# Where ScalarE and VectorE read the keys of two urgent searches in an attention and mixture-of-experts kernel

## The chip, the cores and the metric

The kernel runs on one core of one Trainium2 chip. The metric is the device time of one execution in microseconds (us). A core has engines that each work off their own instructions in order and wait for one another through semaphores: TensorE (PE; its weight loads are PEld), VectorE (DVE), ScalarE (ACT), GpSimd (POOL) and SyncE (SP), which issues transfers. SBUF is the large memory on the core, PSUM the small one into which TensorE writes its sums.

## The reference

Three layers follow one another:

```python
a = softmax(causal(q @ k.T / 8)); local = a @ v            # 4 batches, 8 heads, 576 rows, 64 columns
mem_out = (phi(q) @ M_prev) / (phi(q) @ z_prev + 1e-6)     # phi(x) = elu(x) + 1
x = g * mem_out + (1 - g) * local                          # 2304 tokens of 512

logits = x @ w_gate                                        # 8 experts
for idx in argsort(-logits.flatten()):                     # greedy, best pair of token and expert first
    tok, e = idx // 8, idx % 8
    if assigned[tok] >= 0 or counts[e] >= 288: continue    # each expert takes 2304 / 8 tokens
    assigned[tok] = e; counts[e] += 1
out[assigned == e] = relu(x[mask] @ w1[e]) @ w2[e]         # per expert, 512 -> 1024 -> 512

out = (silu(x @ w_gate2) * (x @ w_val)) @ w_out            # 512 -> 1536 -> 512
```

The greedy assignment is what the change is about: which expert fills up first, and with which 288 tokens, has to be known before that expert's products can start.

## The kernel before, in words

**The attention** fills the first 250 us. Then come eight routings, one for each expert in the order in which the experts fill up; each is followed by the expert's products, and after every 512 tokens the last layer runs for that group of tokens (four groups of 512 and one of 256).

**A routing** (`route`, from L990) takes each token's wish (its best open expert), turns the 18 x 8 values so that 8 rows per expert hold 160 keys each (`vb`, `kx`, L1009 to L1022), and searches the 288th largest key of each expert. The search goes by digits of base 4, 16 rounds, eight on the upper 16 bits of the key (`t.h[1]`, L1035) and eight on the lower ones; between the halves (L1094) the lower bits (`t.h[0]`, L1039) are added to what is left of the upper ones. In a round three thresholds are tried: ScalarE counts for the first with a Sign (L1050, L1052; result in `sg`), VectorE for the other two (L1060, L1063; result in `cn`); TensorE adds up the counts over the rows of an expert (L1076, L1077, with `grp` and `ngrp`); VectorE compares with 288 and adds the digit (L1081) to what was found. After 16 rounds the key is turned on TensorE (L1110), the expert that is full first is chosen, the ranks of its tokens are found (L1139 to L1207), and TensorE makes the list of token numbers (L1217), with which GpSimd gathers the tokens (`xg`, L1273) and the weights (`r`).

**The urgent searches** are those of routings 0 and 1 (`near`, which `HARDS = 2` sets). They have their own form. The keys lie in PSUM, in the tile `rp` (`t.pk`, 512 columns of 4 bytes, which is one bank): the keys in columns 0 to 159, what is left of them in the second half in 256 to 415, TensorE's sums from column 480. VectorE counts from there with the digits found so far as an operand (L1060), so that no threshold has to be made first. ScalarE cannot take thresholds in that way; so in each round but the last of a half it copies the keys with the sign turned and the next threshold added (L1071) from `rp` to one of the two SBUF tiles that the keys would otherwise take, and its next Sign (L1050) reads that copy. Rounds 0 and 8 have no found digits: VectorE (L1063) and ScalarE's Sign (L1052) both read `rp`.

**What sets the order.** A planner (`schedule`) takes operations with estimated durations and dependencies and works out one order for each engine, before anything runs. The operations of the urgent searches are marked as hard: others may be put ahead of them on an engine only if they end in time by the estimates. Between them the planner puts other work. In the first search there are only conversions of the last layer's weights from 64-bit floats (`from64`): ScalarE makes two parts (L434, L440), VectorE shifts one (L442) and puts the sign to it in two halves (L445), GpSimd adds (L448). 34 of these remain after the attention. In the second search there are also the products of expert 0 (L1255): the turning of its tokens (L1486, L1489, L1491), the splitting of weights into a high and a low part (`ws`: ScalarE L1284, then VectorE or GpSimd L1288), and `hd` (L1517, L1519). Ahead of expert 0 stand four groups of products that only keep TensorE busy (L1300).

[...]

Of the kernel before, what the change touches and what calls it, by code (L numbers as in the profile page):

```python
# [74 lines left out]
def kernel(ctx: ExitStack, tc: tile.TileContext, qt_, kt_, v, M_prev, z_prev, beta,  # L75
# [910 lines left out]
    def route(ph, prev):  # L986
# [6 lines left out]
        def step(eng, dur, fn, deps=(), **kw):  # L993
            last[0] = Op(None, {eng: dur}, fn, deps=[last[0]] + list(deps), hard=ph < HARDS, **kw)
            return last[0]
# [29 lines left out]
        def f(e):  # L1025
            t.h = [rt.tile([128, 160], F32, name=f"h{x}") for x in range(3)]
            t.kd = rt.tile([128, 2], F32, name="kd")
            t.junk = rt.tile([128, 160], BF, name="junk")
            t.jk2 = rt.tile([128, 160], BF, name="jk2")
            t.kj = rt.tile([128, 16], F32, name="kj")  # L1030
            if near:

                ptile()
                t.pk, t.hs, t.h[1] = t.p, list(t.h), t.p[:, 0:160]
            A.activation(t.h[1], t.kx.bitcast(U16).rearrange("p (c b) -> p b c", b=2)[:, 1], AF.Copy)  # L1035
            t.R = t.h[1]
        near, sk, base = ph < HARDS, rp(), None
# [5 lines left out]
        for rd in range(16):  # L1043
            sp_ = sk if near else rp()
            past = near and rd % 8 > 0

            def f(e, rd=rd, past=past):
                with nc.allow_low_precision(reason="whole numbers up to 160"):
                    if past:
                        A.activation(t.jk2, t.xs, AF.Sign, bias=gain[:, rd, 3:4], accum_out=sgns[rd % 2])  # L1050
                    else:
                        A.activation(t.jk2, t.R, AF.Sign, scale=-1.0, bias=t.th[:, 0:1] if rd % 8 else steps[:, rd, 0:1],  # L1052
                                     accum_out=sgns[rd % 2])
            sgn = Op(None, {"A": 0.49}, f, deps=[last[0], base], hard=near, lat=SAFE if ph else 0.0, slack=RND if ph else 0.0,
                     use=[sk] if near and not past else [])

            def f(e, rd=rd, past=past):
                for j in (1, 2):
                    if past:
                        V.scalar_tensor_tensor(t.junk, t.R, gain[:, rd, 3:4], steps[:, rd, j:j + 1].to_broadcast([128, 160]),  # L1060
                                               op0=OP.subtract, op1=OP.is_ge, accum_out=cnts[rd % 2][:, j:j + 1])
                    else:
                        V.tensor_scalar(t.junk, t.R, t.th[:, j:j + 1] if rd % 8 else (j + 1) * 4.0 ** (7 - rd), None,  # L1063
                                        op0=OP.is_ge, op1=OP.add, accum_out=cnts[rd % 2][:, j:j + 1])
            cnt = step("V", 0.8 if past else 0.74 if rd % 8 else 0.6, f, lat=SAFE if ph else 0.0, slack=RND if ph else 0.0,
                       use=[sk] if near else [])
            if near and (rd + 1) % 8:

                def f(e, rd=rd):
                    t.xs = t.hs[1 + rd % 2]  # L1070
                    A.activation(t.xs, t.R, AF.Copy, scale=-1.0, bias=4.0 ** (6 - rd) - (0.5 if rd < 8 else 2.0 ** -17))  # L1071
                base = Op(None, {"A": 0.24}, f, deps=[sgn], hard=True, use=[sk])

            def f(e, rd=rd):
                t.p = t.pk[:, 480 + 16 * (rd % 2):] if near else ptile()
                PE.matmul(t.p[:, 0:4], grp, cnts[rd % 2], start=True, stop=False)  # L1076
                PE.matmul(t.p[:, 0:1], ngrp, sgns[rd % 2], start=False, stop=True)  # L1077
            step("PE", 0.08, f, deps=[sgn], take=[] if near else [sp_], use=[sk] if near else [])

            def f(e, rd=rd):  # L1080
                V.scalar_tensor_tensor(t.kj[:, 0:4], t.p[:, 0:4], float(CAP), gain[:, rd], op0=OP.is_ge, op1=OP.mult,  # L1081
                                       accum_out=gain[:, rd + 1, 3:4] if (rd + 1) % 8 else t.kd[:, 1 - rd // 8:2 - rd // 8])
            step("V", 0.17, f, use=[sp_])
            if (rd + 1) % 8 and not near:
                def f(e, rd=rd):
                    t.th = rt.tile([128, 4], F32, name="th", bufs=2)
                    V.tensor_scalar(t.th[:, 0:3], steps[:, rd + 1], gain[:, rd + 1, 3:4], None, op0=OP.add, op1=OP.add,
                                    accum_out=t.th[:, 3:4])
                step("V", 0.22, f)
            elif rd == 7:  # L1090
                def f(e):
                    if near:
                        t.h[2] = t.pk[:, 256:416]
                    V.scalar_tensor_tensor(t.h[2], t.h[1], t.kd[:, 1:2], t.h[0], op0=OP.subtract, op1=OP.add)  # L1094
                    t.R = t.h[2]
                step("V", 0.35 if near else 0.25, f, deps=[low_], port="" if near else "V", use=[sk] if near else [])

        def f(e):
            t.key = rt.tile([128, 2], U16, name="key")
# [550 lines left out]
```

## Time and profile before

| what | value |
|---|---|
| three runs | 1043.67, 1036.31, 1039.59 us, median 1039.59 |
| the profiled execution | 1039.32 us |
| its span, first to last instruction | 1037.6 us |
| TensorE, matmuls | busy 923.2 us, 89% of the span |
| VectorE | busy 783.5 us, 76% |
| ScalarE | busy 598.6 us, 58% |
| GpSimd | busy 312.2 us, 30% |
| granted TensorE clock, mean | 0.944 of full speed |
| chain that ended last | TensorE 71%, VectorE 17%, ScalarE 7% |

A busy engine is one that has an instruction under way. The share is a mean over stages with different limits: in the first search TensorE is all but idle, in the last layer it is full. [...] Idle time is put down to the engine and line that ended it, which the profile infers from semaphores; a wait for several is put down to the last of them. Line numbers in the tables are those of the kernel before; the changed kernel has them one to three lines further down.

### The profile page before, as it was taken

The page shows a single profiled execution, that of the slowest core. Times are in us where ns is not written, and L with a number is a line of the kernel's source. Part 1 is how long each engine was busy: PE and PEld are TensorE (multiplying, and loading weights), DVE is VectorE, ACT ScalarE, POOL GpSimd, SP SyncE. Part 2 cuts the span into 40 slices and gives each one's busy share as a digit, 9 for nine tenths or more (in the row PEclk, how much of TensorE's full clock was granted, in tenths as well). Part 3 has the DMA queues.
Part 4 walks back from the last instruction along what each step waited for, and adds up shares of the span by engine and source line. Part 5 has one row for each costly group of instructions (what it writes and reads, how often), then busy time and mean ns, then how long its engine had stood idle before and what let it go on. Part 6 is the DMA issues. An engine that isn't in the chain of part 4 may idle for free.

```text
span 1037.6 us, 19343 instructions
## 1 busy us (share of the span) xinstructions
PE 923.2 (89%) x6917; PEld 785.0 (76%) x6917; DVE 783.5 (76%) x2575; ACT 598.6 (58%) x1331; POOL 312.2 (30%) x432
## 2 busy tenths in 40 slices
PE   6779989885168789998999999999999999999995
PEld 3558778774047787776998778899778899888895
DVE  6987888895877999998988777878787765443562
ACT  5878879862646477457465445466445455333552
POOL 3567677841243433153520110320011230000200
PEclk9999899998558899999999999999999999999998
DMA  8499698675351533172340120340030250000100
GB/s 243 101 195 220 133 217 189 138 164 148 101 188 59 185 123 102 61 246 82 120 149 1 38 105 4 118 149 1 1 123 24 67 180 21 1 1 1 42 1 20
DMA packets 128160, 105.37 MB, mean 102 GB/s; under 512 B 96752, under 2 KB 110208, under 8 KB 126016
## 3 DMA queue, kind: packets, MB, share of 16 engines
q1 hardware_dynamic: 118176, 61.14, 24.5%
q0 software_dynamic: 9888, 43.00, 12.4%
q8 instruction: 54, 0.88, 0.4%
q14 instruction: 42, 0.34, 0.1%
HBM read 72.39 MB, written 9.45 MB: 79 GB/s over the span
## 4 chain that ended last, share of the span: by engine, by line
PE 71%; DVE 17%; ACT 7%; issue 2%; DMA 1%; POOL 1%; ACTq 0%; SPq 0%; DVEq 0%; POOLq 0%
PE wkp L1255 37%; PE acc L1255 21%; PE sp L673 3%; PE O L842 2%; DVE ws L1288 2%; ACT P L723 2%; DVE nm L709 2%; DVE junk L1060 1%; PE T L971 1%; PE wkp L1486 1%; DVE f64a L445 1%; DVE nm L707 1%; PE T L902 1%; PE T L807 1%; ACT P L718 1%
## 5 line engine op out<-in xcount | busy, mean ns | idle before, releaser
L1255 PE MATMUL wkp<-ya,ws 128*128 128x512 f32 (+1 forms) x864 | 179.7, 361 | 2.7 <-DVE xt L1491 2.2
L1288 DVE TENSOR_TENSOR ws<-m2r,ws 128x512 fp32r<-128x512 f32 x166 | 115.6, 696 | 69.8 <-ACT ws L1284 67.5
L1255 PE MATMUL acc<-ws,us 128*128 128x512 f32 x648 | 162.1, 394 | 0.0
L1255 PEld LDWEIGHTS wkp<-ya,ws 128*128 128x128 f32 x864 | 142.0, 190 | 24.1 <-issue 2.2
L1284 ACT ACTIVATE ws<-m2r 128x512 fp32r<-128x512 f32 x170 | 106.6, 628 | 80.3 <-PE wkp L1255 41.6
L1255 PE MATMUL wkp<-yb,ws 128*128 128x512 f32 x576 | 137.8, 393 | 0.0
L1255 PEld LDWEIGHTS acc<-ws,us 128*128 128x128 f32 x648 | 118.4, 188 | 22.1
L1255 PE MATMUL wkp<-xt,ws 128*128 128x288 f32 x768 | 122.1, 308 | 3.0 <-DVE ws L1288 2.6
L1255 PEld LDWEIGHTS wkp<-yb,ws 128*128 128x128 f32 x576 | 106.4, 188 | 21.0
L1255 PE MATMUL acc<-hd,ws 128*128 128x288 f32 x768 | 120.1, 304 | 1.7 <-DVE hd L1519 0.7
L1255 PEld LDWEIGHTS wkp<-xt,ws 128*128 128x128 f32 x768 | 111.0, 197 | 3.6 <-DVE ws L1288 2.9
L1255 PEld LDWEIGHTS acc<-hd,ws 128*128 128x128 f32 x768 | 109.0, 193 | 3.6 <-DVE hd L1519 1.5
L781 POOL TENSOR_TENSOR pb<-P,pb 128x576 f16<-128x576 f32 (+2 forms) x61 | 92.9, 1525 | 48.0 <-ACT pb L774 39.5
L1284 ACT ACTIVATE ws<-r 128x512 fp32r<-128x512 f32 x128 | 80.0, 647 | 40.8 <-PE acc L1255 15.1
L1288 DVE TENSOR_TENSOR ws<-r,ws 128x512 fp32r<-128x512 f32 x122 | 87.5, 730 | 15.8 <-ACT ws L1284 14.0
L448 POOL TENSOR_TENSOR m2r<-f64a,f64r 128x512 int32<-128x512 int32 x34 | 45.5, 1339 | 113.6 <-DVE f64a L445 45.7
L1366 ACT ACTIVATE sil<-wkp 128x512 f32<-128x512 f32 (+1 forms) x60 | 33.2, 553 | 74.8 <-PE wkp L1255 54.9
L1409 POOL DMA_INDIRECT out_dram<-f64r,gi x18 | 22.6, 1254 | 172.0 <-DVE f64r L1402 119.4
L1273 POOL DMA_INDIRECT r<-in_moe_w_dram,wi x32 | 33.9, 1060 | 127.7 <-DVE key L1100 72.9
L673 PE MATMUL sp<-kt,qt 64*128 64x288 f32 (+4 forms) x576 | 57.8, 329 | 14.8 <-ACT P L718 8.8
L1063 DVE TENSOR_SCALAR_CACHE_REDUCE junk<-h,th 128x160 bf16<-128x160 f32 x168 | 63.5, 378 | 4.9
L673 PEld LDWEIGHTS sp<-kt,qt 64*128 64x128 f32 x576 | 47.0, 198 | 24.6 <-ACT P L718 11.3
(245 smaller groups left out, 1651.8 us busy)
## 6 DMA issues: line engine op xcount, KB each, us to landing
f<-in_moe_w_out_dram SPq DMA_DIRECT2D x12, 512.0 KB
f<-in_moe_w_gate_dram SPq DMA_DIRECT2D x11, 512.0 KB, 5.9
f<-in_moe_w_val_dram SPq DMA_DIRECT2D x11, 512.0 KB, 3.6
vr<-in_vb_dram SPq DMA_DIRECT2D x16, 320.0 KB, 3.3
xq<-in_qt_dram SPq DMA_DIRECT2D x16, 288.0 KB, 4.1
xk<-in_kt_dram SPq DMA_DIRECT2D x16, 288.0 KB, 4.2
xs<-X SPq DMA_DIRECT2D x3, 1024.0 KB
pt<-pb SPq DMA_TRANSPOSE x49, 3.5
```

Source lines behind the costliest of these rows:

```text
L448: return op({"G": 1.225}, lambda e: G.tensor_tensor(dst.bitcast(I32), t.a, t.r, op=OP.add), [o1] + o4, use=[ra, aa])
L673: PE.matmul(dst, st, mv, start=k not in keys[:j], stop=k not in keys[j + 1:])
L709: V.tensor_reduce(nm[:, i], sp[0][:, :, o:o + w], axis=AX.X, op=OP.max, negate=True)
L723: A.activation(p.P[m][:, q0 + w * s:q0 + w * s + w], sp[0][:, s, o:o + w], AF.Exp, bias=nm[:, i, s:s + 1])
L781: lambda e, i=i, c=c: (V if e == "V" else G).tensor_tensor(p.pb[i][:, 1, c], p.P[i][:, c], p.pb[i][:, 0, c], op=OP.subtract), deps=[ho], u ...
L1063: V.tensor_scalar(t.junk, t.R, t.th[:, j:j + 1] if rd % 8 else (j + 1) * 4.0 ** (7 - rd), None, op0=OP.is_ge, op1=OP.add, accum_out=cnts[r ...
L1255: PE.matmul(dst, st(x), mv(y), start=first and t == 0, stop=last and t == 2)
L1273: G.indirect_dma_start(out=dst, out_offset=None, in_=src, in_offset=bass.IndirectOffsetOnAxis(ap=idx, axis=0))
L1284: A.activation(h.t[:, 0], raw(), AF.Copy)
L1288: (V if e == "V" else G).tensor_tensor(h.t[:, 1], raw(), _f(h.t[:, 0]), op=OP.subtract)
L1366: A.activation(t.sl, t.g[0][:, 0:n], AF.Silu)
L1409: put = G.indirect_dma_start(out=out, out_offset=bass.IndirectOffsetOnAxis(ap=self.gi[:, q:q + 1], axis=0), in_=t.o, in_offset=None)
```

## The change

In the urgent searches the keys are written to SBUF (`t.h[1]`) first. ScalarE's Sign and its copies read them there. Rounds 0 and 8 count from SBUF on both engines; in each of them ScalarE, behind its Sign, writes a copy of the keys into PSUM (`t.RP`, columns 0 to 159 in round 0, 128 to 287 in round 8), and VectorE's counts of the other rounds read that. The two SBUF tiles for ScalarE's copies are no longer two of the three `h` tiles, but the routing's first tiles, `vb` and `kx`, which are free by then; the first copy must therefore come behind the reading of the lower bits out of `kx` (`low_`). What is left of the keys after the first half (L1094 before) goes to SBUF. [...]

```diff
             if near:
 
                 ptile()
-                t.pk, t.hs, t.h[1] = t.p, list(t.h), t.p[:, 0:160]
+                t.pk, t.hs = t.p, [t.vb, t.kx.bitcast(F32)]
             A.activation(t.h[1], t.kx.bitcast(U16).rearrange("p (c b) -> p b c", b=2)[:, 1], AF.Copy)
             t.R = t.h[1]
...
                         A.activation(t.jk2, t.R, AF.Sign, scale=-1.0, bias=t.th[:, 0:1] if rd % 8 else steps[:, rd, 0:1],
                                      accum_out=sgns[rd % 2])
-            sgn = Op(None, {"A": 0.49}, f, deps=[last[0], base], hard=near, lat=SAFE if ph else 0.0, slack=RND if ph else 0.0,
+                    if near and not past:
+                        t.RP = t.pk[:, 16 * rd:16 * rd + 160]
+                        A.activation(t.RP, t.R, AF.Copy)
+            sgn = Op(None, {"A": 0.49 if past or not near else 0.84}, f, deps=[last[0], base], hard=near, lat=SAFE if ph else 0.0, slack=RND if ph else 0.0,
...
                     if past:
-                        V.scalar_tensor_tensor(t.junk, t.R, gain[:, rd, 3:4], steps[:, rd, j:j + 1].to_broadcast([128, 160]),
+                        V.scalar_tensor_tensor(t.junk, t.RP, gain[:, rd, 3:4], steps[:, rd, j:j + 1].to_broadcast([128, 160]),
...
-                    t.xs = t.hs[1 + rd % 2]
+                    t.xs = t.hs[rd % 2]
                     A.activation(t.xs, t.R, AF.Copy, scale=-1.0, bias=4.0 ** (6 - rd) - (0.5 if rd < 8 else 2.0 ** -17))
-                base = Op(None, {"A": 0.24}, f, deps=[sgn], hard=True, use=[sk])
+                base = Op(None, {"A": 0.32}, f, deps=[sgn, low_], hard=True)
...
-            step("PE", 0.08, f, deps=[sgn], take=[] if near else [sp_], use=[sk] if near else [])
+            step("PE", 0.01 if near else 0.08, f, deps=[sgn], take=[] if near else [sp_], use=[sk] if near else [])
...
                 def f(e):
-                    if near:
-                        t.h[2] = t.pk[:, 256:416]
                     V.scalar_tensor_tensor(t.h[2], t.h[1], t.kd[:, 1:2], t.h[0], op0=OP.subtract, op1=OP.add)
                     t.R = t.h[2]
-                step("V", 0.35 if near else 0.25, f, deps=[low_], port="" if near else "V", use=[sk] if near else [])
+                step("V", 0.39 if near else 0.25, f, deps=[low_], port="V")
```

The change moves instructions at three places of which the prediction speaks. The first is ScalarE at the start of the first search (rounds 0 to 2), before:

```order
L1035 ACTIVATE rp<-kx 128x160
L1052 ACTIVATE jk_4709,sg_155<-rp,steps 128x160
L1071 ACTIVATE h_4705<-rp 128x160
L1039 ACTIVATE h_4704<-kx 128x160
L1050 ACTIVATE jk_4709,sg_156<-h_4705,gain 128x160
L1071 ACTIVATE h_4706<-rp 128x160
L440 ACTIVATE f64a<-f_4690 128x512
```

and in the changed kernel:

```order
L1035 ACTIVATE h_4705<-kx 128x160
L1052 ACTIVATE jk_4709,sg_155<-h_4705,steps 128x160
L1056 ACTIVATE rp<-h_4705 128x160
L1039 ACTIVATE h_4704<-kx 128x160
L1074 ACTIVATE vb<-h_4705 128x160
L1050 ACTIVATE jk_4709,sg_156<-vb,gain 128x160
L1074 ACTIVATE kx<-h_4705 128x160
L440 ACTIVATE f64a<-f_4690 128x512
```

The keys go to SBUF, the copy into `rp` (L1056) is new, the lower bits (L1039) come ahead of the first copy for the Sign (L1074), and these copies read and write SBUF alone.

The second place is TensorE in rounds 1 and 2 of the first search, with what it waits for, before:

```order
L1076 MATMUL rp<-cn_154,grp 128x4 [waits Activation_49]
L1077 LDWEIGHTS ngrp
L1077 MATMUL rp<-sg_156,ngrp 128x1
L1076 LDWEIGHTS grp
L1076 MATMUL rp<-cn_153,grp 128x4 [waits Activation_49]
```

and in the changed kernel:

```order
L1079 MATMUL rp<-cn_154,grp 128x4 [waits DVE_49]
L1080 LDWEIGHTS ngrp
L1080 MATMUL rp<-sg_156,ngrp 128x1 [waits Activation_49]
L1079 LDWEIGHTS grp
L1079 MATMUL rp<-cn_153,grp 128x4 [waits DVE_49]
```

The sum of the counts waited for ScalarE (which itself had waited for VectorE); now it waits for VectorE, and the sum of the Sign for ScalarE.

The third place is TensorE behind the second routing's list of tokens (the last of its 18 products, L1217 before, L1218 now), up to the first products of expert 1, before:

```order
L1217 MATMUL rp<-tk,so 96x3
L1255 MATMUL acc<-hd,ws 128x288 x12
L1255 MATMUL wkp<-xt,ws 128x288 x12
L1255 MATMUL acc<-hd,ws 128x288 x24
L1486 MATMUL wkp<-ident,xg 128x96 x3
L1009 MATMUL rp<-ident,vw 128x128
L1449 MATMUL wkp<-ident,ixf 3x96
L1486 MATMUL wkp<-ident,xg 128x96 x9
L1255 MATMUL wkp<-xt,ws 128x288 x27
```

and in the changed kernel:

```order
L1218 MATMUL rp<-tk,so 96x3
L1256 MATMUL acc<-hd,ws 128x288 x24
L1009 MATMUL rp<-ident,vw 128x128
L1450 MATMUL wkp<-ident,ixf 3x96
L1487 MATMUL wkp<-ident,xg 128x96 x12
L1079 LDWEIGHTS grp
```

Of expert 0's 192 products 48 stood behind this routing and 24 stand there now; the other 24 stand ahead of it, between the rounds of its search.

## Rows read from the trace of the kernel before

**Rows 1.** The page's first line: the span of the execution.
```profile
span 1037.6 us, 19343 instructions
```
**Rows 2.** Stages: us, busy time (and instructions) of each engine, TensorE clock, DMA share, GB/s.
```profile
257.00:285.00 28.00, 3.08 (x33) 2.20 (x32) 21.95 (x115) 19.79 (x59) 6.45 (x10) 0.50 0.30 94
...
307.00:320.00 13.00, 8.38 (x50) 7.72 (x49) 10.55 (x36) 7.83 (x24) 9.44 (x14) 0.76 0.32 105
320.00:335.00 15.00, 15.00 (x103) 14.42 (x103) 9.52 (x52) 11.98 (x35) 1.67 (x3) 0.83 0.12 36
...
395.00:470.00 75.00, 74.28 (x365) 57.52 (x364) 69.13 (x261) 44.19 (x100) 26.76 (x37) 1.00 0.43 139
```
**Rows 3.** Timeline, round 4 of the first search: start, us, engine, line, operation [idle before].
```profile
262.66 0.16 DVE L1081 SCALAR_TENSOR_TENSOR kj<-rp,gain 128x4 f32<-128x4 f32 x1
...
263.30 0.38 DVE L1060 SCALAR_TENSOR_TENSOR junk<-rp,gain,steps 128x160 bf16<-128x160 f32 x1
...
263.79 0.30 ACT L1071 ACTIVATE h<-rp 128x160 f32<-128x160 f32 x1 [0.40 <-DVE junk L1060]
...
264.14 0.16 PE L1076 MATMUL rp<-cn,grp 128*128 128x4 bf16 x1 [1.59 <-ACT h L1071]
...
264.45 0.16 DVE L1081 SCALAR_TENSOR_TENSOR kj<-rp,gain 128x4 f32<-128x4 f32 x1
```
**Rows 4.** Timeline, round 7, the last of a half.
```profile
268.66 0.38 DVE L1060 SCALAR_TENSOR_TENSOR junk<-rp,gain,steps 128x160 bf16<-128x160 f32 x1
...
269.34 0.16 DVE L1081 SCALAR_TENSOR_TENSOR kj<-rp,gain 128x4 f32<-128x4 f32 x1
```
**Rows 5.** Timeline, round 0: the Sign, its read-out, and round 1's first count.
```profile
255.39 0.39 ACT L1052 ACTIVATE jk<-rp,steps 128x160 bf16<-128x160 f32 x1
255.69 0.20 ACT L1052 ACTIVATION_READ_ACCUMULATOR jk<-rp,steps 128x1 bf16 x1
...
257.51 0.38 DVE L1060 SCALAR_TENSOR_TENSOR junk<-rp,gain,steps 128x160 bf16<-128x160 f32 x1
```
**Rows 6.** Timeline, the step between the halves, and round 9's first count.
```profile
269.55 0.39 DVE L1094 SCALAR_TENSOR_TENSOR rp<-rp,kd,h 128x160 f32<-128x160 f32 x1
...
272.02 0.38 DVE L1060 SCALAR_TENSOR_TENSOR junk<-rp,gain,steps 128x160 bf16<-128x160 f32 x1
```
**Rows 7.** Lines L1052 and L1063: ns min/median/max, first and last start us.
```profile
L1052 ACT ACTIVATE jk<-h,steps x12: 412/430/441, 358.3 to 789.8; 128x160 bf16<-128x160 f32 x12
...
L1052 ACT ACTIVATE jk<-rp,steps x4: 394/394/396, 255.4 to 315.7; 128x160 bf16<-128x160 f32 x4
...
L1063 DVE TENSOR_SCALAR_CACHE_REDUCE junk<-h x24: 308/320/322, 358.9 to 790.1; 128x160 bf16<-128x160 f32 x24
...
L1063 DVE TENSOR_SCALAR_CACHE_REDUCE junk<-rp x8: 323/324/325, 255.9 to 315.2; 128x160 bf16<-128x160 f32 x8
```
**Rows 8.** Timeline of the second search, and the line of VectorE's splits.
```profile
306.92 3.24 PE L1255 MATMUL wkp<-xt,ws 128*128 128x288 f32 x12
...
315.48 4.05 DVE L1288 TENSOR_TENSOR ws<-r,ws 128x512 fp32r<-128x512 f32 x1
...
335.48 0.22 PE L1110 MATMUL rp<-ident,sg 8*128 8x8 f32 x1
...
352.36 0.49 PE L1486 MATMUL wkp<-ident,xg 96*128 96x96 f32 x3
...
L1288 DVE TENSOR_TENSOR ws<-r,ws x122: 676/689/4050, 295.3 to 867.1; 128x512 fp32r<-128x512 f32 x122
```
**Rows 9.** Groups by line, 250 to 540 us: busy us, mean ns, idle us before.
```profile
L445 DVE SCALAR_TENSOR_TENSOR f64a<-f,f64a 128x256 int32<-128x256 int32 x68 | 33.0, 509 | 0.1
...
L440 ACT ACTIVATE f64a<-f 128x512 f32<-128x512 f32 x34 | 22.3, 660 | 2.7 <-POOL spacer L404 1.7 <-DMA f<-in_moe_w_val_dram 1.0
...
L442 DVE TENSOR_SCALAR f64a<-f64a 128x512 int32<-128x512 int32 x34 | 16.1, 480 | 0.0
...
L1288 POOL TENSOR_TENSOR ws<-r,ws 128x512 fp32r<-128x512 f32 x6 | 7.7, 1279 | 10.0 <-ACT ws L1284 10.0
```

## The prediction

> **What bounds the kernel now.** I read four views, from coarse to fine. The page gives the span, 1037.6 us [rows 1]; the profiled execution took 1039.32 us, so 1.72 us lie around the span, and the median of the three runs, 1039.59, is 0.27 above it. The table by stage [rows 2] shows where TensorE isn't full. From 257 to 285 us, the first urgent search, it works 3.08 of 28 us at a granted clock of 0.50; VectorE is busy 21.95 us there. From 307 to 320 it works 8.38 of 13 us, while from 395 to 470 it works 74.28 of 75. So what happens before the middle of the span shifts everything behind it, as long as VectorE (69.13 of 75 us in 395 to 470) keeps up.
>
> The timeline of one search round [rows 3] shows a chain over three engines: VectorE's second count starts at 263.30 and lasts 0.38, to 263.68; only then ScalarE's copy of the keys (L1071) starts, at 263.79; it ends at 264.09; TensorE sums at 264.14; VectorE takes the digit (L1081) at 264.45. From digit to digit (262.66 to 264.45) are 1.79 us. The copy reads keys that lie in the PSUM tile that VectorE counts from and that TensorE writes its sums to, and all three take turns. The last round of a digit half has no copy [rows 4]: its second count ends at 269.04 and the digit follows at 269.34. From end of count to digit that is 0.30 instead of 0.77 us.
>
> **The change, part by part.**
>
> *The copy leaves the chain.* Its source is in SBUF now, so TensorE waits for the counts first (the order's waits, second place shown above) and the copy runs beside them. Twelve rounds of a search (1 to 6, 9 to 14) have a copy behind VectorE's PSUM counts; each should shrink by 0.77 - 0.30 = 0.47 us: 12 x 0.47 = 5.6 us. What covers the copy is the counts. The round that is left, 1.79 - 0.47 = 1.32 us, must hold ScalarE's sign (0.50, from [rows 5]), its copy (0.30) and, in about eight rounds, a conversion of 0.66 [rows 9]: 1.46 us, so at worst 0.14 too much in eight rounds, 1.1 us; at best nothing, since the ends of ScalarE's instructions overlap the next ones and the sign may come later than the counts. Conversions that VectorE fits into its gap I cost at nothing: TensorE's sum covers them.
>
> *Rounds 0 and 8.* In round 0 the sign starts at 255.39 and round 1's count at 257.51 [rows 5]: 2.12 us, since sign, counts and copy take turns. In the change the counts (2 x about 0.37, from 0.32 us instructions) run beside the sign, 0.50 us; then ScalarE writes the keys into PSUM. That copy stands in no row; the nearest is the copy the other way, 0.30 [rows 3], and I take that, with 0 and twice that as bounds. From a copy's end to the digit are 0.36 (264.09 to 264.45), from a digit to VectorE's next work 0.21 (269.34 to 269.55). 0.50 + 0.30 + 0.36 + 0.21 = 1.37 us: 0.75 saved. Round 8 ran from 269.55 to 272.02 [rows 6], 2.47 us; now 0.42 for the subtraction, about 0.03 to the sign, then the same 1.37: 1.82, so 0.65 saved. Sum for the first search: 5.6 + 0.75 + 0.65 = 7.0 us, less 0.2 because VectorE now does two halves of a conversion behind the last digit where one instruction stood: **6.8 us**, with ends 5.1 (ScalarE too late, both new copies double) and 7.4 (both hidden).
>
> *Reading from the other memory.* ScalarE's sign takes 394 ns from PSUM and 430 from SBUF; VectorE's count 324 and 320 [rows 7]. Only rounds 0 and 8 change memory for these, so that is 36 ns twice a search, beside the counts: nothing on the path. [...]
>
> *From the first search to expert 0.* What follows the search (gathers, four warm-up groups on TensorE, turning of the tokens) keeps its length; only the rounds 0 to 4 of the second search, which stand in TensorE's queue between these, get shorter. I take 0.7 us (0 to 1.5: below, the warm-ups and the gather end as before; above, three rounds' 0.47). Expert 0's first product, at 306.92, should start near 299.4.
>
> *The second search* runs under expert 0's products. Where twelve products stand between two rounds, TensorE is full (15.00 of 15 us in 320 to 335, 103 instructions [rows 2]), and a shorter round gains nothing. The order moves 24 products from behind this routing to ahead of it (third place shown above): at 15.00/103 = 0.146 us each, 3.5 us later for the routing. Against that stands TensorE's idle time in 307 to 320, 4.6 us, which shorter rounds can take back in part. From expert 0's first product to the transpose of the found key are 28.6 us now [rows 8]; I expect 28.6 + 3.5 - 2.0 = 30.1. Behind the routing 48 products stand ahead of expert 1's tokens, which TensorE turns at 352.36; with 24 there, the tokens needn't wait for products, and I take 1.5 us back (nothing to 3.5, the 24 products themselves). So the second search and what moves with it come out at **0 us** (+3.5 - 2.0 - 1.5), with ends +3.5 (nothing back) and -4.6 (all of the 4.6 and 3.5 back).
>
> *The backlog.* The first search has less idle time, so fewer conversions of the last layer's weights fit: in the order, 13 of the 34 precede the first multiplication of the last layer on VectorE, 16 before. A conversion is one shift and two halves there, 16.1/34 + 33.0/34 = 1.4 us with stalls [rows 9]; three are 4.3 us. They go into the last layer, where VectorE has 5.9 us idle in 395 to 470. In expert 0 three splits (median 0.69 us [rows 8]) go from VectorE to GpSimd, 1.28 us each there [rows 9], which gives VectorE 2.1 us back. I take 1.0 us of loss, nearer to nothing because the 2.1 come first (0 to 4.3).
>
> Sum: -6.8 - 0.7 + 0 + 1.0 = **-6.5 us**; against its own execution 1039.32 - 6.5 = 1032.8, and with the median's 0.27, **1033 us**.
>
> **The rivals.** Main case: the first search's gain reaches the end, 1029 to 1036; 0.56.
>
> *The second search shrinks too.* If the stall at 315.48 (a split of VectorE that takes 4.05 us against a median of 0.69 [rows 8], while GpSimd works too) vanishes with the new timing and the rounds before it take their 0.47, up to 4.6 us come on top; with the other terms at their better ends the sum is -7.4 - 1.5 - 4.6 = -13.5: 1026 to 1029. For it: the stall is chance of timing. Against it: TensorE is full behind it, and 24 more products stand ahead. 0.18.
>
> *Conversions come late.* VectorE and TensorE are both near full from 395 us on; if the three conversions are late for the products that read them, each costs its 1.4 us and TensorE waits: 4.3 us lost in place of 1.0, 1036.4, and with the first search at its poorer end (5.1) 1038: 1036 to 1039. For it: 69.13 of 75 us. Against it: splits moved off VectorE. 0.18.
>
> *Slower: GpSimd holds VectorE up.* The changed order gives GpSimd 16 splits where it had 11, and the row at 315.48 shows the price: VectorE's 0.69 became 4.05 us, 3.36 more, which is 2.6 of GpSimd's splits of 1.28. Five more that each hold VectorE for their whole length cost 6.4 us; with three late conversions (4.3) the loss is 10.7 against a gain of 7.5: 1042.5. It decides from a loss of 7.5 us on, about six such splits; slower by over 1% would take some 14. Against it: the planner keeps these apart, and single splits mostly cost nothing. 0.05, of which 0.02 over 1%.
>
> *The change doesn't do what it says.* VectorE still counts in the tile that TensorE writes sums to, so a wait could stay. The order shows TensorE waiting for the counts rather than the copy; a round of 1.79 us would have to remain for another reason: 1039. 0.03.
>
> **How the numbers follow.** The likeliest is the main case, 1033. The range takes in the main case, late conversions, and the upper half of the second search's case: 1027 to 1039. A measurement of this kernel can tell about 1%, 10.4 us, from no change. Faster by more, below 1029: nearly all of the second search's case, 0.18. Slower by more: 0.02 to 0.03. The rest, 0.79, lies within 1%; a gain of two thirds of a per cent is the forecast.
>
> **What would show it.** In the first search: rounds of 1.3 us in place of 1.79, TensorE's sum released by VectorE's count, not by the copy; rounds 0 and 8 near 1.4 and 1.8; the last digit some 7 us earlier. Expert 0's first product near 299.4; expert 1's tokens turned near 345.5 in place of 352.36; TensorE still full from about 388 on. Wrong would be: rounds at 1.6 or more (ScalarE or a conversion ends them), VectorE's splits at over 2 us in expert 0, or TensorE waiting for converted weights between 430 and 490.

## The result, and the profile after

The changed kernel takes 1027.12 us (median of 17 runs, 1025.55 to 1034.37) against 1039.59 for the kernel before in the same series; the ratio is 0.990, 95% interval 0.988 to 0.992. In a second series it took 1030.21 (12 runs), ratio 0.9935, interval 0.991 to 0.996. So the gain is 7 to 12 us. 1033 had been forecast, with a range of 1027 to 1039. The profiled execution took 1029.43 us. Its page begins:

```profile
span 1027.7 us, 19331 instructions
...
PE 920.5 (90%) x6917; PEld 783.2 (76%) x6917; DVE 778.1 (76%) x2569; ACT 598.5 (58%) x1336; POOL 320.1 (31%) x442
```

The four stages of [rows 2] again (us, busy time and instructions by engine, granted clock, DMA). The first three are moved to where they lie now; the last is moved by 7 us only:

```profile
257.00:278.00 21.00, 2.69 (x28) 1.89 (x27) 19.18 (x100) 16.04 (x52) 4.16 (x6) 0.50 0.24 75
300.00:313.00 13.00, 12.33 (x83) 11.34 (x82) 8.45 (x40) 10.23 (x31) 9.25 (x13) 0.87 0.33 119
313.00:328.00 15.00, 14.80 (x117) 13.83 (x115) 11.79 (x64) 10.79 (x32) 5.50 (x8) 1.00 0.11 36
388.00:463.00 75.00, 69.75 (x332) 53.32 (x331) 68.60 (x264) 44.21 (x100) 31.40 (x41) 0.96 0.45 149
```

The first search still runs at a clock of 0.50, but is over sooner (by 5.6 us, see the table of marks below). Behind expert 0's first product TensorE is busy 12.33 of 13 us where it was busy 8.38, and in the two stages there the clock is 0.87 and 1.00 where it was 0.76 and 0.83. The last row is worse: in the last layer TensorE was full (74.28 of 75 us), now it is busy 69.75. (The layer itself has moved by 13.7 us; at the same distance from its first product, 381.3 to 456.3, TensorE is busy 71.05 of 75.)

One round, as in [rows 3] (timeline: start, us, engine, line, operation, idle before):

```profile
258.31 0.16 DVE L1084 SCALAR_TENSOR_TENSOR kj<-rp,gain 128x4 f32<-128x4 f32 x1
...
258.95 0.38 DVE L1063 SCALAR_TENSOR_TENSOR junk<-rp,gain,steps 128x160 bf16<-128x160 f32 x1
259.00 0.32 ACT L1074 ACTIVATE kx<-h 128x160 f32<-128x160 f32 x1
...
259.40 0.16 PE L1079 MATMUL rp<-cn,grp 128*128 128x4 bf16 x1 [1.13 <-DVE junk L1063]
...
259.63 0.16 DVE L1084 SCALAR_TENSOR_TENSOR kj<-rp,gain 128x4 f32<-128x4 f32 x1
```

From digit to digit are 1.32 us, where they were 1.79. ScalarE's copy (L1074) runs at 259.00 beside VectorE's second count (258.95), and what releases TensorE's sum is VectorE's count. The step between the halves [rows 6], however, looks like this:

```profile
263.95 1.26 POOL L448 TENSOR_TENSOR m2r<-f64a,f64r 128x512 int32<-128x512 int32 x1 [22.61 <-DVE kj L1084]
...
264.54 0.95 DVE L445 SCALAR_TENSOR_TENSOR f64a<-f,f64a 128x256 int32<-128x256 int32 x1
...
265.57 1.26 POOL L448 TENSOR_TENSOR m2r<-f64a,f64r 128x512 int32<-128x512 int32 x1 [0.34 <-DVE kj L1084]
265.61 1.40 DVE L1095 SCALAR_TENSOR_TENSOR h<-h,kd,h 128x160 f32<-128x160 f32 x1
...
267.55 0.29 ACT L1056 ACTIVATE rp<-h 128x160 f32<-128x160 f32 x1
...
268.40 0.38 DVE L1063 SCALAR_TENSOR_TENSOR junk<-rp,gain,steps 128x160 bf16<-128x160 f32 x1
```

VectorE's subtraction takes 1.40 us in place of 0.39: it starts 0.04 us behind GpSimd's second addition and ends 0.18 us behind its end (267.01 against 266.83). The half of a conversion ahead of it (L445), beside the first addition, took 0.95 us against a median of 0.42 of its line. The marks of [rows 8] now, on TensorE's timeline: expert 0's first product, the second key, expert 1's tokens (the first of which waits for its gather), and the last layer's first product:

```profile
300.28 0.76 PE L1256 MATMUL wkp<-xt,ws 128*128 128x288 f32 x2
...
325.20 0.22 PE L1111 MATMUL rp<-ident,sg 8*128 8x8 f32 x1
...
338.89 0.28 PE L1487 MATMUL wkp<-ident,xg 96*128 96x96 f32 x1
339.73 0.36 PE L1487 MATMUL wkp<-ident,xg 96*128 96x96 f32 x1 [0.56 <-DMA xg<-xs,ix]
...
375.06 0.85 PE L1256 MATMUL wkp<-ya,ws 128*128 128x512 f32 x3
```

What lies ahead of the routing differs from execution to execution, though no kernel here changes it: the first turn of the gate values (L1009) starts between 250.0 and 257.6 us. So marks are compared below as us behind that turn, each kernel from its one profile; the second column alone counts from the start of the span. "End" is the last instruction. The kernels from the third row on are described under Experiments.

| kernel | first turn at | first key | expert 0's first product | second key | expert 1's tokens | last layer | end | last layer to end |
|---|---|---|---|---|---|---|---|---|
| before | 253.44 | 31.55 | 53.48 | 82.04 | 98.92 | 135.36 | 784.2 | 648.8 |
| after | 252.67 | 25.95 | 47.61 | 72.53 | 86.22 | 122.39 | 775.0 | 652.6 |
| after, again | 255.25 | 25.89 | 47.61 | 72.57 | 86.32 | 122.49 | 775.2 | 652.7 |
| order alone | 252.04 | 31.36 | 55.61 | 81.71 | 95.21 | 130.17 | 783.4 | 653.2 |
| memory alone | 253.24 | 27.08 | 47.85 | 75.20 | 92.12 | 128.57 | 777.4 | 648.8 |
| first search alone | 257.62 | 25.82 | 50.15 | 78.57 | 94.31 | 130.27 | 783.8 | 653.5 |
| second search alone | 254.41 | 31.56 | 52.57 | 77.81 | 94.44 | 133.01 | 782.7 | 649.7 |
| all keys in SBUF | 251.84 | 26.80 | 49.36 | 76.71 | 91.05 | 125.84 | 780.3 | 654.4 |
| other slices read | 250.65 | 25.95 | 47.14 | 70.54 | 84.63 | 119.35 | 771.8 | 652.4 |
| shifts left out | 252.52 | 25.94 | 47.61 | 72.56 | 86.24 | 122.93 | 772.0 | 649.0 |
| less lead | 250.03 | 25.95 | 47.53 | 70.96 | 85.27 | 120.96 | 772.1 | 651.1 |
| other plan | 250.13 | 25.95 | 47.63 | 72.34 | 86.48 | 119.95 | 771.8 | 651.8 |
| true rounds | 251.81 | 24.10 | 45.81 | 65.70 | 83.77 | 116.56 | 772.9 | 656.3 |
| true rounds, other plan | 255.24 | 24.11 | 45.62 | 66.09 | 84.47 | 116.82 | 774.4 | 657.5 |

How far such marks can be trusted: after, its repetition, "other slices read" and "shifts left out" have one order up to the last layer. Up to expert 0's first product they agree within 0.5 us, at the last layer three of them within 0.6, and one is 3 us earlier: a difference of up to 3 us between two single profiles shows nothing there. From the last layer to the end the first three agree within 0.3; the fourth leaves work out in that stretch.

### The profile page after: what moved, and what is told of

The parts are those of the page before. It is cut to its first block, busy times and chain, and to the rows that moved or that the text cites. A ratio compares the mean times of both kernels' runs of the same rounds, so it can differ in the third digit from the quotient of the medians.

```text
span 1027.7 us, 19331 instructions
## 1 busy us (share of the span) xinstructions
PE 920.5 (90%) x6917; PEld 783.2 (76%) x6917; DVE 778.1 (76%) x2569; ACT 598.5 (58%) x1336; POOL 320.1 (31%) x442
## 3 DMA queue, kind: packets, MB, share of 16 engines
q1 hardware_dynamic: 118176, 61.14, 24.9%
## 4 chain that ended last, share of the span: by engine, by line
PE 69%; DVE 17%; ACT 7%; issue 3%; POOL 2%; DMA 2%; SPq 0%; ACTq 0%; DVEq 0%; POOLq 0%
PE wkp L1256 37%; PE acc L1256 22%; PE sp L673 2%; PE O L842 2%; ACT P L723 2%; DVE ws L1289 2%; DVE nm L709 2%; DVE f64a L445 1%; DVE junk L1063 1%; PE T L971 1%; DVE junk L1066 1%; PE wkp L1487 1%; PE T L807 1%; DVE nm L707 1%; PE T L902 1%
## 5 line engine op out<-in xcount | busy, mean ns | idle before, releaser
L1289 DVE TENSOR_TENSOR ws<-r,ws 128x512 fp32r<-128x512 f32 x119 | 82.6, 704 | 15.7 <-ACT ws L1285 13.3
L1410 POOL DMA_INDIRECT out_dram<-f64r,gi x18 | 20.5, 1138 | 166.9 <-DVE f64r L1403 119.4
```

The lines of the kernel that those rows point to most:

```text
L1289: (V if e == "V" else G).tensor_tensor(h.t[:, 1], raw(), _f(h.t[:, 0]), op=OP.subtract)
```

## Experiments

**Order and memory apart.** The change moves data and also tells the planner other durations, which makes another order. Order alone:

```
 sgn = Op(None, {"A": 0.49 if past or not near else 0.84}, ...)
 base = Op(None, {"A": 0.32}, f, deps=[sgn, low_], hard=True)
 step("PE", 0.01 if near else 0.08, ...)
 step("V", 0.39 if near else 0.25, f, deps=[low_], port="V")
 (on the kernel before; keys and turned keys where they were)
```

> The kernel before with the changed kernel's durations in the planner alone: the order of the instructions is the changed one (153 products ahead of the second search's found key, 16 splits on GpSimd), but the keys and the turned keys lie where they lay before. Theory A (the gain is the copy's leaving the chain, in both searches): rounds of the first search stay at 1.79 us, the key of the second search is found about 28.6 + 3.5 = 32 us behind expert 0's first product, time 1038 to 1043. Theory B (half of the gain is the order: the 4.05 us stall at 315.48 is gone, splits are on GpSimd): rounds stay at 1.79, but the key comes about 25 us behind expert 0's first product, and the time is about 1039.6 - 6 = 1033.5 us.

1040.97 us (10 runs), ratio 1.0016, interval 0.9987 to 1.0045: no gain. Yet neither theory had it right. The marks show a gain of 5.2 us up to the last layer (135.36 to 130.17), all of it behind expert 0's first product (which itself comes 2.1 us later), and 4.4 us given back from the last layer to the end. Memory alone, that is the change with the four old durations:

> The changed kernel's places in memory with the old durations in the planner: the order of the instructions is the one before (129 products ahead of the second key, 11 splits on GpSimd). Theory A: rounds of 1.32 us and a last digit some 6.4 us earlier, and the second search shrinks too; with 24 products fewer ahead of its key it comes at least as early behind expert 0's first product as in the changed kernel (24.9 us), time 1026 to 1030. Theory B: the first search's gain alone, 1033 us, and the second key about 28 us behind expert 0's first product.

1031.71 us (5 runs), ratio 0.9914, interval 0.988 to 0.995. Up to the last layer 6.8 us are gained (5.6 of them ahead of expert 0's first product), and nothing is given back (648.8). By time this kernel can't be told from the whole change (0.990 and 0.9935 in its two series): what the order gains and gives back comes out near nothing, and the data paths alone make the gain. From first product to second key are 27.35 us, which is theory B's 28 and not A's 24.9. The reason stands in VectorE's timeline of this kernel:

```profile
309.14 4.30 DVE L1289 TENSOR_TENSOR ws<-r,ws 128x512 fp32r<-128x512 f32 x1
```

and in GpSimd's:

```profile
309.09 1.29 POOL L1289 TENSOR_TENSOR ws<-r,ws 128x512 fp32r<-128x512 f32 x1
...
310.35 1.30 POOL L1289 TENSOR_TENSOR ws<-r,ws 128x512 fp32r<-128x512 f32 x1
...
311.63 1.26 POOL L1289 TENSOR_TENSOR ws<-r,ws 128x512 fp32r<-128x512 f32 x1
```

The stall of 4.05 us of [rows 8] is there again, behind shorter rounds: it belongs to the old order. In the new order VectorE's longest split in that stage is 1.12 us (order alone) and 1.08 (after). What the order does to TensorE shows in the table by stage. From first product to second key, before:

```profile
306.90:335.50 28.60, 23.98 (x154) 22.58 (x153) 20.57 (x86) 20.42 (x58) 11.11 (x16) 0.80 0.21 67
```

and after:

```profile
300.30:325.20 24.90, 24.29 (x177) 22.82 (x178) 17.35 (x85) 20.41 (x60) 14.73 (x20) 0.93 0.23 79
```

24 products more stand in the stretch, TensorE is busy 0.3 us longer, idles 0.6 us instead of 4.6, and its granted clock is 0.93 instead of 0.80. With order alone the clock is 0.92, too. Before, the granted clock fell while TensorE waited for VectorE's long split: it was 1.00 in 316 to 318 us, 0.59 in 318 to 319, where TensorE did nothing, and 0.50 in 319 to 320. Here are the row behind that wait and the two pieces of 4 us around its end:

```profile
319.59 1.81 PE L1255 MATMUL wkp<-xt,ws 128*128 128x288 f32 x6 [2.63 <-DVE ws L1288]
```
```profile
316.00:320.00 4.00, 0.97 (x6) 0.74 (x6) 3.96 (x5) 1.22 (x6) 3.76 (x7) 0.77 0.38 123
320.00:324.00 4.00, 4.00 (x19) 3.86 (x19) 2.42 (x12) 3.19 (x11) 0.35 (x1) 0.50 0.44 131
```

TensorE worked 0.97 of 4 us at a mean clock of 0.77; then it was busy for all of the next 4 us at 0.50 and got through 19 instructions. At 1.00 it got through 34 in as long, after:

```profile
304.00:308.00 4.00, 4.00 (x34) 3.83 (x33) 2.72 (x14) 2.88 (x10) 2.33 (x5) 1.00 0.09 12
```

What the clock alone is worth shows a kernel with the same order up to here ("other slices read" below): it had 1.00 for the whole stretch, and its products took 22.81 us in place of 24.29:

```profile
297.80:321.20 23.40, 22.81 (x178) 21.42 (x178) 17.34 (x85) 20.36 (x60) 14.54 (x20) 1.00 0.28 95
```

**One search at a time.** A flag that is true for routing 0 (or 1) chooses the new form:

```
+new = ph == 0            # second run: ph == 1
-if near and not past:
+if new and not past:
 (and so at the turned keys, the counts' source, the subtraction, the four durations)
```

> The change in the first urgent search alone (the second as before). Theory A: rounds of 1.32 us in the first search, first product of expert 0 6 to 7 us earlier, the second search at its old length (28 us or more from first product to key): 1039.6 - 6.5 = 1033 us. Theory B (the order makes the second half of the gain, and here 15 of the 24 products have moved and GpSimd has 14 splits): below 1031 us.

1038.69 us (10 runs), ratio 1.0002, interval 0.997 to 1.0035. The first search is as short as in the change (25.82), but expert 0's first product comes only 3.3 us earlier than before, where the change has 5.9: the rounds that stand ahead of it in TensorE's queue are those of the old second search. From first product to second key it keeps the old 28.4 us, as A said. Up to the last layer 5.1 us are gained, and behind that mark 4.7 given back, as in the order alone. Both theories missed the time, since neither had the last layer's loss.

> The change in the second urgent search alone, with the order of the kernel before there (129 products ahead of the key, 11 splits on GpSimd). Theory A: the first search as before, then from expert 0's first product to the second key 4 us less than 28.6, time 1039.6 - 4 to 6 = 1033.5 to 1035.5 us. Theory B (the second search is hidden under TensorE's products, its rounds cost nothing): 1039 us.

1038.56 us (10 runs), ratio 0.9997, interval 0.997 to 1.002. From first product to second key 25.24 us, 3.3 less than before, near A's 4; but of the second key's 4.2 us only 2.4 are left at the last layer, less than these marks can tell, and 1.5 at the end. A's time was wrong and B's right, though B's reason (rounds that cost nothing) was not what the marks show.

**VectorE in SBUF too.**

```
-t.RP = t.pk[:, 16 * rd:16 * rd + 160]
-A.activation(t.RP, t.R, AF.Copy)
+t.RP = t.R
```

> The changed kernel without the copy of the keys into PSUM: VectorE counts from SBUF too, so nothing but the sums lies in the PSUM tile; the rest and the order stay. Theory A (what counts is that ScalarE is out of the tile; where VectorE reads is all one): rounds stay at 1.32 us, rounds 0 and 8 lose at most 0.3 us each, time 1026 to 1027.5. Rival (VectorE must read in PSUM, or GpSimd's additions, 1.26 us each, hold its counts up): counts beside an addition take 1 us or more in place of 0.32, the first search is 1 to 4 us longer, time 1028 to 1031.

1034.59 us (10 runs), ratio 0.9995, interval 0.996 to 1.003: no gain that can be told from noise, though the marks keep 3.9 of the 9.2 us. The first key comes 0.9 us later than in the change (26.80), from first product to second key are 27.35 us in place of 24.92, and from the last layer to the end it takes 1.8 us more. The counts' line (ns min/median/max, first and last start), here

```profile
L1062 DVE SCALAR_TENSOR_TENSOR junk<-h,gain,steps x56: 372/385/1900, 255.0 to 326.2; 128x160 bf16<-128x160 f32 x56
```

and in the changed kernel

```profile
L1063 DVE SCALAR_TENSOR_TENSOR junk<-rp,gain,steps x56: 376/384/386, 255.9 to 322.9; 128x160 bf16<-128x160 f32 x56
```

The median is the same, the longest is 1900 ns against 386. In the timeline of the SBUF variant, GpSimd's

```profile
316.39 1.29 POOL L1288 TENSOR_TENSOR ws<-r,ws 128x512 fp32r<-128x512 f32 x1 [1.62 <-PE rp L1079]
...
319.47 1.43 POOL L1288 TENSOR_TENSOR ws<-r,ws 128x512 fp32r<-128x512 f32 x1
```

and VectorE's

```profile
316.68 1.19 DVE L1062 SCALAR_TENSOR_TENSOR junk<-h,gain,steps 128x160 bf16<-128x160 f32 x1
...
317.92 0.39 DVE L1062 SCALAR_TENSOR_TENSOR junk<-h,gain,steps 128x160 bf16<-128x160 f32 x1
...
319.87 1.20 DVE L1062 SCALAR_TENSOR_TENSOR junk<-h,gain,steps 128x160 bf16<-128x160 f32 x1
```

The two counts that started beside one of these splits took 1.19 and 1.20 us and ended 0.19 and 0.17 us behind its end; the one between them took 0.39. So GpSimd's work holds counts up, as the rival had it; its time was too low, since most of the loss lies behind the first search. In the changed kernel, with the keys in PSUM (one operand, the steps, is in SBUF still), no count took over 386 ns, though GpSimd has the same splits: the two at 317.20 and 317.63 took 0.38 us each beside a split of 1.32 us at 316.90. Why a count from SBUF is held, these rows don't show.

**What the last layer gives back.** TensorE there, in the changed kernel:

```profile
453.38 0.49 PE L1487 MATMUL wkp<-ident,xg 96*128 96x96 f32 x3
454.59 0.18 PE L1079 MATMUL rp<-cn,grp 128*128 128x4 bf16 x1 [0.71 <-DVE junk L1066]
...
456.69 0.18 PE L1079 MATMUL rp<-cn,grp 128*128 128x4 bf16 x1 [1.46 <-DVE junk L1066]
...
457.52 1.22 PE L1256 MATMUL wkp<-ya,ws 128*128 128x512 f32 x2 [0.63 <-ACT ws L1285]
459.02 7.26 PE L1256 MATMUL wkp<-ya,ws 128*128 128x512 f32 x20 [0.28 <-DVE ws L1289]
```

Two rounds of the fourth search (the expectations call it the third, whose key came at 409.57) and the turning of expert 2's tokens stand ahead of the products, and the products wait for a split; behind the gap 20 of them take 7.26 us, 0.36 each. The ninth step of the layer, from SiLU to SiLU on ScalarE, takes 17.5 us:

```profile
446.18 0.57 ACT L1367 ACTIVATE sil<-wkp 128x512 f32<-128x512 f32 x1
...
463.69 0.60 ACT L1367 ACTIVATE sil<-wkp 128x512 f32<-128x512 f32 x1 [0.65 <-PE wkp L1256]
```

and with the old order (memory alone) 7.2:

```profile
454.28 0.57 ACT L1367 ACTIVATE sil<-wkp 128x512 f32<-128x512 f32 x1
...
461.48 0.58 ACT L1367 ACTIVATE sil<-wkp 128x512 f32<-128x512 f32 x1
```

Not all of these 10.3 us are lost: the next two steps take 12.2 and 7.4 us, with the old order 13.8 and 10.4. Is the converted weight late? Here the products read weights that were ready:

```
+def known(k, n): return m2(n - 18 if k == 0 and n >= 20 else n)
-split(lambda ...: m2(3 * f + w), ...)
+split(lambda ...: known(self.k, 3 * f + w), ...)
```

> The changed kernel, same order of instructions, but in the last layer's first group the products that would read slices 20 to 35 of the converted weights read slices 2 to 17, which were converted long before; all conversions are still made. (This changes what is computed.) Theory A (TensorE waits there for late conversions): from the layer's first product to the end 648.5 us or less in place of 652.6, the ninth step 8 to 11 us in place of 17.5, time 1023 us. Rival (the engines' time there is simply used up, the conversions are not what is waited for): 652 us, time 1027.

1030.69 us (10 runs), ratio 0.9947, interval 0.992 to 0.997. From the last layer to the end 652.4, the ninth step 17.1 us. Theory A falls: with the data there the gap stays. Is it VectorE's work itself, then, or the order?

```
-lambda e: V.tensor_scalar(t.a, t.a, 3, None, op0=OP.logical_shift_left)
+lambda e: V.tensor_scalar(t.a, t.a, 3, None, op0=OP.logical_shift_left) if n < 14 else None
```

> The changed kernel, same order of instructions, without VectorE's shift (0.43 us each) in the conversions of the slices from 14 on, some 21 of them, which stand in the last layer's first group. (This changes what is computed.) It takes about 9 us of work off VectorE there. Theory C (VectorE's time is used up in the last layer's first group, so every conversion that didn't fit ahead is paid for): from the layer's first SiLU to the end 648.4 us falls to 645 us or less, the ninth step to 12 us or less. Theory D (the loss is in the order of the queues: the ninth step's products stand in TensorE's queue behind three rounds of the third search and behind the turning of tokens): 647.5 us or more, the ninth step 16 us or more.

1027.23 us (4 runs), ratio 0.987, interval 0.980 to 0.9935. From the first SiLU (379.74) to the end (1024.5) are 644.8 us against 648.4: C's 645, and the 644.5 of the kernel before. But the ninth step takes 15.9 us, near D's 16:

```profile
445.83 0.60 ACT L1367 ACTIVATE sil<-wkp 128x512 f32<-128x512 f32 x1
...
461.76 0.60 ACT L1367 ACTIVATE sil<-wkp 128x512 f32<-128x512 f32 x1
```

Each theory is half right: taking 9 us of VectorE's work off gives 3.6 back, spread over steps 8 to 11, but the gap stays where it was. The traces have more on this: the number of half conversions (L445, two to a conversion) that stand behind the last layer's first product, before and in the changed kernel (ns min/median/max, first and last start):

```profile
L445 DVE SCALAR_TENSOR_TENSOR f64a<-f,f64a x39: 409/419/1508, 391.6 to 494.0; 128x256 int32<-128x256 int32 x39
```
```profile
L445 DVE SCALAR_TENSOR_TENSOR f64a<-f,f64a x45: 408/419/2034, 378.1 to 484.5; 128x256 int32<-128x256 int32 x45
```

The time from there to the end goes with this number in all kernels of the table that make every conversion whole. With 39 or 40 (before, memory alone, second search alone) it is 648.8 to 649.7 us; with 44 to 46 (after and its repetition, order alone, first search alone, all keys in SBUF, other slices read, less lead, other plan) 651.1 to 654.4; with 48 (the two kernels with true rounds) 656.3 and 657.5. So the loss goes with the conversions left to do. How much of it an order could save with the same number left stays open; the next runs tried.

**Other orders with the same data paths.** One planner constant:

```
-RSL, SSL, CSL, PRESS, ROUTE0 = 15, 0.5, 0, 3, 60
+RSL, SSL, CSL, PRESS, ROUTE0 = 10, 0.5, 0, 3, 60
```

> The changed kernel with one constant of the planner changed: the lead that it gives the later routings' addresses falls from 15 to 10, so the third search takes VectorE's time later and the conversions that the last layer waits for stand earlier in VectorE's queue. Theory A (the changed order gives 4 us back in the last layer because slices of its weights, the 28th above all, are converted late): the ninth step of the last layer no longer takes 17.5 us, from the layer's first product to the end are 649 to 650 us in place of 652.6, time 1027.1 - 3 = 1024 us. Rival (the loss there has another cause, such as VectorE held up by GpSimd): 652 us or more, time 1027.

1029.33 us (9 runs), ratio 0.9916, interval 0.988 to 0.995; the ninth step 12.6 us, but from the last layer to the end still 651.1, between the two theories.

```
-RSL, CSL, XAT, WAITP, AHEAD, RND = 15, 0, 9, 0.4, 6, 1.5
+RSL, CSL, XAT, WAITP, AHEAD, RND = 10, 4, 8, 0.3, 4, 1.0
```

Six constants, not the five that the expectation counts:

> The changed kernel with five constants of the planner changed (leads of routings and conversions, how far TensorE may run ahead, where expert tokens are turned): conversions of the last layer's weights earlier by some 12 us from the 25th slice on, 147 products ahead of the second key. Theory A: the last layer takes 649 us or less from its first product to the end, and its first product comes as early as in the changed kernel (122 us behind the first turn): 1021 to 1024 us. Rival (the loss in the last layer is not from late conversions): 1027 us.

1026.08 us (4 runs), ratio 0.9917, interval 0.9885 to 0.995; 651.8 there, the rival's side. The lower median is within what two series of the changed kernel differ by.

```
-cnt = step("V", 0.8 if past else 0.74 ...)
+cnt = step("V", 0.6 if past else 0.74 ...)
```

> The changed kernel, with the planner told a round of 1.33 us (0.6 for the two counts in place of 0.8), as the trace shows, in place of 1.53. Theory A (GpSimd's additions land on VectorE's steps because the plan runs slower than the chip): in the first search no step of VectorE takes over 0.8 us, the first search's key comes 24.5 us behind the first turn in place of 25.95 and the second turn 35 to 36 us behind it in place of 38.1; but fewer conversions fit ahead (26 rows of them in place of 36), so the last layer is 2 to 4 us longer: 1023 to 1027 us. Rival (additions collide wherever they are planned): 25.95 and 38.1 us as before, 1027 to 1031 us.

1029.23 us (6 runs), ratio 0.992, interval 0.989 to 0.995. The first half of A holds: first key at 24.10, second turn at 34.7 us (38.1 in the changed kernel), and up to the second turn no instruction of VectorE takes over 0.75 us, where the changed kernel has 1.40 and 1.76. Up to the last layer 5.8 us are gained on the change; from there 3.7 given back (656.3). With three other constants besides:

```
-RSL, CSL, XAT = 15, 0, 9
+RSL, CSL, XAT = 10, 8, 7
```

> As the run with the planner's round at 1.33 us, with less lead for the later routings' addresses (10 in place of 15), more for the conversions (8 in place of 0) and the next expert's tokens turned two steps earlier in the last layer. Theory A (the last layer's loss is written into the order, by splits and products that stand behind the third search's rounds): the last layer takes 649 to 652 us from its first product to the end, and with the first search's gain the time is 1018 to 1022 us. Rival (the loss cannot be planned away): 653 us or more there, 1024 to 1027 us.

1029.87 us (12 runs), ratio 0.9935, interval 0.991 to 0.996; from the last layer's first product to the end 657.5. The rival holds, and more: 5.7 us gained ahead, 4.9 back. On the same chip, the changed kernel:

> The changed kernel once more, on the same chip as the two others, so that they can be held against it: ratio to the kernel before 0.988 to 0.992; from the last layer's first product to the end 652 to 653 us, from the first turn to it 121 to 123 us by every theory.

1030.21 us (12 runs), ratio 0.9935; marks as in the first profile within 0.1 us, and the ratio is past what was expected (0.988 to 0.992), though its interval, 0.991 to 0.996, reaches into that. No other order can be told from it by time.

## Why the prediction was right, and where it was wrong

*The copy leaves the chain: right.* Rounds of 1.32 us, as worked out, and TensorE released by the count. The first key comes 5.6 us earlier where 6.8 was forecast: two of GpSimd's additions hold VectorE up, by 1.0 us at the subtraction and 0.5 at the conversion. The prediction had that mechanism only in its slower rival, as splits in the second search at up to 1.28 us each; additions in the first search it put at nothing. The other memory cost nothing on the path, as forecast: ScalarE's copies take 0.32 us in place of 0.30.

*Rounds 0 and 8: right.* Round 0 is 1.28 us (1.37 forecast), the new copy 0.29 (0.30). Round 8 is 2.79, and 1.78 without the 1.01 of the stall (1.82 forecast).

*To expert 0's first product: nearly.* 5.9 us in all, where 7.5 was forecast. Between the second turn and the first product 2.0 us came back, where 0.7 had been taken (0 to 1.5; memory alone gives 1.2 there). A third addition of GpSimd took most of it. One of VectorE's instructions that took 0.20 us before takes 1.76 and ends 0.07 us behind the addition's end, though it began 0.43 us ahead of it by these rows:

```profile
282.38 1.76 DVE L1174 TENSOR_TENSOR cum<-cum,pn 128x36 f32<-128x36 f32 x1
```
```profile
282.81 1.26 POOL L448 TENSOR_TENSOR m2r<-f64a,f64r 128x512 int32<-128x512 int32 x1
```

*The second search: wrong, the step that failed.* "TensorE is full (15.00 of 15 us in 320 to 335), and a shorter round gains nothing", with 24 products at 0.146 us making 3.5 us more: 0 us in all. Measured: -7.1 us (3.6 up to the second key, 3.2 behind it, 0.3 to the last layer). The two terms that were mis-sized are the 3.5 us for the products, which cost 0.3 us of busy time, and the 2.0 us of idle time taken back, which is 4.0 (4.6 to 0.6). Full was read without the clock beside it: 15.00 us at 0.83. With the long wait gone, the clock over the stretch is 0.93 in place of 0.80. And the stall at 315.48 is no chance of timing but part of the old order: it is there with memory alone, and gone with order alone. The two runs apart put 7.3 us of this on the order (74.56 from first product to last layer, before 81.88; 2.1 of them because its first product comes later) and 1.2 on the shorter rounds, the latter less than what marks can tell. That the second search shrinks was a rival at 0.18, but it took the stall for chance and the shorter rounds for the other cause.

*The backlog: mechanism right, size wrong.* 1.0 us was taken of 0 to 4.3; it was 3.8, with three conversions more behind the layer's first product, as forecast. The 2.1 us that splits on GpSimd were to give back to VectorE could not be set against them: the three splits lie ahead of the last layer (VectorE has 23 there in place of 26, and 96 behind in both kernels). TensorE waiting for converted weights between 430 and 490 had been named as the sign; it does wait there, but the run with other slices shows that the converted data is not what it waits for.

The sum by the marks: -5.6 - 0.3 - 7.1 + 3.8 = -9.2 us (784.2 to 775.0), against -6.5. Two rivals came true at once and partly cancelled. So it is luck in part that the time lies within the range, by 0.1 us at its lower end (and at 1030.21 in the second series). What was forecast, the first search's gain that reaches the end, is what memory alone makes: -6.8 us by the marks. The sign of 345.5 for expert 1's tokens leaves out the 0.7 us that the prediction's own terms add (344.9); they came 12.7 us earlier by the marks. That ScalarE must leave the tile, memory alone shows; that VectorE must not follow it into SBUF, the SBUF variant.

## What to carry to other kernels

Where engines take turns on one PSUM tile, try giving a reader its own memory (a round fell from 1.79 to 1.32 us here), and look in its new place at how long its instructions take beside those of a third engine (beside a split of GpSimd VectorE's counts took 1.19 and 1.20 us from SBUF, 0.38 from PSUM). Where a change also alters a planner's costs, run the order and the data paths apart: here the order gained 5 us and gave back 4, which no diff shows. A TensorE that is busy 100% of a stage at a granted clock below 1 may have room: here it got through 103 instructions in 15.00 us at 0.83, and through 117 in 14.80 us at 1.00 once the wait ahead of the stage was gone. And time saved ahead of a stage that another engine nearly fills may be lost again there, as 3.8 us were here, with VectorE busy 68.60 of 75 us.

## What the runs showed of the hardware that was not expected

One instruction of VectorE lasted through three of GpSimd's in a row: with memory alone a split that began at 309.14 took 4.30 us (the median of such splits before is 0.69) and ended at 313.44, while GpSimd ran splits of 1.29, 1.30 and 1.26, the second and third of which began at 310.35 and 311.63, with only a memset of 0.09 ahead of each, and the last ended at 312.89. An instruction with a single tensor as its input was held as well: with all keys in SBUF, one of VectorE's shifts (median 0.42 us in the changed kernel) took 1.16 at 318.60, beside a split on GpSimd (318.13, 1.34 us). VectorE's counts took as long from PSUM as from SBUF (medians of 384 ns and 385), while ScalarE's copy was 0.02 us longer from SBUF than from PSUM (0.32 against 0.30).
